# A 64-point transform centred on 31.5, so that the back-transform gives even and odd rows and one product gives a point and its mirror

## The chip, the cores and the metric

The kernel runs on one core of a Trainium2 chip. The metric is the device time of one execution in microseconds. Engines are named as in the profile: PE is the tensor engine's matmul, PEld its weight load, DVE the vector engine, ACT the scalar engine, POOL GpSimd, SP the engine whose queue issues most of the transfers.

## What is computed

```python
X = np.fft.rfft(x, axis=1)                       # x: 2 x 3008 x 256, float32
y = np.fft.irfft(X * (filt_r + 1j * filt_i)[None], n=3008, axis=1)
t = y.reshape(6016, 256)
g = t @ w_gate                                   # 256 x 1536
t = (g / (1 + np.exp(-g)) * (t @ w_val)) @ w_out # 1536 x 256
h = t @ w_in                                     # 256 x 2048
out = (h * np.clip(h + 3.0, 0.0, 6.0) / 6.0) @ w_out2
```

A long convolution along the sequence by way of the Fourier transform, and then two gated MLPs on the 6016 tokens that come out of it.

## The kernel before

**The transform.** 3008 is 47 x 64, and the two factors have no common divisor, so the transform splits into one of 47 points (N1) and one of 64 points (N2) without twiddle factors. Only 24 of the 47 frequencies of the first axis are kept (NK), since the input is real. The constants of all these transforms lie in one tile `mat` of 128 partitions, the same in both halves of 64 partitions.

The work runs in 16 steps (2 batches, 8 groups of 32 channels). A step `k` goes through four functions:

- `over_n1` (L414): the 47-point transform on PE, 32 products with 48 rows of contraction and 64 columns of weights; ACT copies the two result banks into `first` (L427, L428), with a negated copy of the real part.
- `over_n2` (L430): the 64-point transform on PE, eight products of 64 x 64 weights and 384 moving columns, four for the cosine and four for the sine, into two banks.
- `filter_product` (L440): DVE multiplies both banks with the real and the imaginary filter into `u` and `v` (L449, four operations of 384 elements); POOL then forms the complex product in place (four operations of 192 elements, through the helpers at L109 and L112).
- `back` (L455): the inverse 64-point transform on PE (L462). Its output rows are 64 real and 64 imaginary ones; each is the sum of a product with the cosine and one with the sine, so eight products of 64 x 64 weights and 384 moving columns. ACT copies the two banks into `turned` (L467).

The array is used as four parts of 64 x 64: a product with weights in rows 0 to 63 or 64 to 127 and results in partitions 0 to 63 or 64 to 127 takes one part, and up to four run beside each other.

The order is written out by hand. In iteration `k` PE's queue gets `over_n1(k)`, `back(k - 2)`, `over_n2(k)`, and in the last two iterations `form(k - 16)` in place of the transforms. The SP queue gets loads of x, filters and the first weights, then (L471) the stores of `turned` to DRAM (`d2`), then (L531) the loads of the first two blocks' data. DVE also decodes the first weights between the steps (`todo`).

**The last sum.** The tokens are worked on in blocks of 512 (the last of a batch 448): 12 blocks in all. For a block, `to_time` (L141) carries the 24 frequencies back to 47 points, on PE (L152). The data comes from DRAM with 48 rows (24 frequencies, real and imaginary) in partitions 0 to 47 for the first 32 values of n2 and the same in 64 to 111 for the other 32. The block's points fall into five to seven turns of at most 47 points. For each half of the channels (128 of 256) and each turn there are four products: two channel quarters of 64 columns, two halves of n2, each with 48 rows of contraction and up to 47 moving columns. They fill two PSUM banks, one for each half of n2. Two splits follow (`time_halves`, L157): ACT casts a bank to the high part of `xs`, DVE subtracts it to get the low part. One split reads both channel halves of its bank.

Blocks 0 and 1 get their last sum in `form` (L535), at the end of the transform stage; there the data of the two channel halves is loaded apart (`load_half`, L527). The other ten get theirs inside the first MLP's loop, at t = 2 * plain - 2 and then once in each block, between the block's `l1` products (L231) and the `l2` products (L243, or L253 in `l2_plain` for the first two blocks).

**The MLPs.** `l1` multiplies with the input weights (128 x 128 weights, 512 or 448 moving columns, in rounded float32 with the weights and the data as sums of two parts), `l2` with the output weights (a scheme of seven products for a 2 x 2 block, 256 or 224 moving columns; 21 products in a step). The order on PE is by hand here too.

Of the kernel before, what the change touches and what calls it, by code (L numbers as in the profile page):

```python
# [16 lines left out]
P = 128  # L17
B, S, D = 2, 3008, 256
N1, N2 = 47, 64
N1P = 48  # L20
NK = 24
# [4 lines left out]
BLOCKS = [(8 * j, min(8, N1 - 8 * j)) for j in range(6)]  # L26
# [20 lines left out]
def _token_times(time):  # L47

    order = []
    for j, n in BLOCKS:  # L50
        n = n * N2 // 2
        for r in range(2):
            q = 32 * j + np.arange(n)
            order.append(time[q % N1, 32 * r + q // N1])
    return np.concatenate(order)


M1, CO, SI, NS, FIN, NM = 0, 48, 112, 176, 240, 288


def _matrices():

    n1, k1, n2 = np.arange(N1), np.arange(NK), np.arange(N2)
    a = 2 * np.pi * (np.outer(n1, k1) % N1) / N1
    b = 2 * np.pi * (np.outer(n2, n2) % N2) / N2
    w = np.where(k1 == 0, 1.0, 2.0)[:, None] / S
    m = np.zeros((2, 64, NM))
    m[:, :N1, M1:M1 + NK] = np.cos(a)
    m[:, :N1, M1 + NK:M1 + 2 * NK] = -np.sin(a)
    m[:, :, CO:CO + N2] = np.cos(b)  # L70
    m[:, :, SI:SI + N2] = np.sin(b)
    m[:, :, NS:NS + N2] = -np.sin(b)
    m[:, 0:2 * NK:2, FIN:FIN + N1] = w * np.cos(a.T)
    m[:, 1:2 * NK:2, FIN:FIN + N1] = -w * np.sin(a.T)
    return np.ascontiguousarray(m.reshape(P, NM), np.float32)


@with_exitstack
def fft_conv_glu_mlp(ctx: ExitStack, tc: tile.TileContext, x, filt, mats, sgn, w1, w2, out):
    nc = tc.nc  # L80
# [9 lines left out]
    mat = keep.tile([P, NM], F32, name="mat")  # L90
# [14 lines left out]
    def bank(tag="gv"):  # L105
        return ps.tile([P, 512], F32, tag=tag, name=tag)

    def minus(out, a, b, engine=None):
        (engine or nc.vector).tensor_tensor(out=out, in0=a, in1=b, op=ALU.subtract)  # L109

    def plus(out, a, b, engine=None):
        (engine or nc.vector).tensor_tensor(out=out, in0=a, in1=b, op=ALU.add)  # L112
# [6 lines left out]
    def rows(i, n=64):  # L119

        return slice(i * 64, i * 64 + n)
# [8 lines left out]
    def load_g(b, j):  # L130
        t0, t1 = turns(*BLOCKS[j][:1], BLOCKS[j][1] * N2)
        g = new_g().rearrange("p (t c) -> p t c", c=D)
        for r in range(2):
            nc.sync.dma_start(out=g[rows(r, N1P), :t1 - t0],
                              in_=d2[b].rearrange("q (h n) c -> (q h) n c", h=2)[:, 32 * r + t0:32 * r + t1])
        return g[:, :, :P], g[:, :, P:]

# [3 lines left out]
    def to_time(g, j, tag="gv"):  # L141

        accs = [bank(tag), bank(tag)]
        first, n = BLOCKS[j][0], BLOCKS[j][1] * N2
        t0, t1 = turns(first, n)
        lo, hi = 32 * first, 32 * first + n // 2
        for a in range(2):
            for t in range(t0, t1):
                i0, i1 = max(lo, t * N1), min(hi, (t + 1) * N1)
                for o in range(0, P, 64):  # L150
                    for r in range(2):
                        nc.tensor.matmul(accs[r][o:o + 64, a * 256 + i0 - lo:a * 256 + i1 - lo],  # L152
                                         g[a][rows(r, N1P), t - t0, o:o + 64],
                                         mat[rows(r, N1P), FIN + i0 - t * N1:FIN + i1 - t * N1])
        return accs

    def time_halves(xs, accs, j, r):  # L157
        n = BLOCKS[j][1] * 32
        src = accs[r].rearrange("p (a n) -> p a n", a=2)[:, :, :n]
        return xs[:, 0, :, r * n:(r + 1) * n], xs[:, 1, :, r * n:(r + 1) * n], src  # L160

# [193 lines left out]
    with tc.manual_schedule():  # L357
# [10 lines left out]
        N = 16  # L368
        STEPS = [(b, 4 * a + i) for a in range(2) for b in range(B) for i in range(4)]
        xin, first, spec, acc2 = {}, {}, {}, {}  # L370
# [69 lines left out]
        def filter_product(k):  # L440

            us = mlp.tile([P, 8, 256], F32, tag="h", name="us").rearrange("p a b -> p (a b)")
            u = us[:, :4 * COLS].rearrange("p (o h n) -> p o h n", o=2, h=2)
            v = us[:, 4 * COLS:8 * COLS].rearrange("p (o h n) -> p o h n", o=2, h=2)
            f = fl[STEPS[k][1] // 4][:, k % 4].rearrange("p r (o n) -> p r o n", o=2)
            for o, acc in enumerate(acc2.pop(k)):
                xa = acc[:, :2 * COLS].rearrange("p (h n) -> p h n", h=2)
                for r, d in enumerate((u, v)):
                    nc.vector.tensor_tensor(out=d[:, o], in0=xa, op=ALU.mult,  # L449
                                            in1=f[:, r, o].unsqueeze(1).to_broadcast([P, 2, COLS]))  # L450
                minus(u[:, o, 0], u[:, o, 0], v[:, o, 1], nc.gpsimd)
                plus(u[:, o, 1], u[:, o, 1], v[:, o, 0], nc.gpsimd)
            spec[k] = u

        def back(k):  # L455

            accs, u = [bank(), bank()], spec.pop(k)
            for m in range(2):
                for h in range(2):
                    w, part = (CO, h) if m == 0 else ((NS, 1), (SI, 0))[h]  # L460
                    for r in range(2):
                        nc.tensor.matmul(accs[r][rows(h), :2 * COLS].rearrange("p (o n) -> p o n", o=2),  # L462
                                         mat[rows(r), w:w + N2], u[rows(r), :, part], start=m == 0, stop=m == 1)
            b, j = STEPS[k]
            to = turned.rearrange("p b q (j r o c) -> p b j r q o c", j=4, r=2, o=2)[:, b, j % 4]
            for r in range(2):
                nc.scalar.copy(out=to[:, r], in_=accs[r][:, :2 * COLS].rearrange("p (o c q) -> p q o c", o=2, q=NK))  # L467
# [59 lines left out]
        def load_half(j, a, g):  # L527
            t0, t1 = turns(*BLOCKS[j][:1], BLOCKS[j][1] * N2)
            g = g[:, :7 * P].rearrange("p (t c) -> p t c", c=P)
            for r in range(2):  # L530
                nc.sync.dma_start(out=g[rows(r, N1P), :t1 - t0],  # L531
                                  in_=d2[0].rearrange("q (h n) c -> (q h) n c", h=2)[:, 32 * r + t0:32 * r + t1, a * P:(a + 1) * P])
            return g

# [39 lines left out]
        hid, accs, late = {}, {}, {}  # L574
        base = 62

        for t in range(2 * n_pair):
            p, i = divmod(t, 2)
            k, g_ = steps[p]
            n, f = ntok(k), 2 * g_ + i  # L580
# [37 lines left out]
            h = hid[p].chunk(i)  # L618
            nc.scalar.activation(out=h, in_=hid[p].halves(gate), func=AF.Silu)  # L619

            lead, rest, part = ([f_ for f_ in range(2, F1) if t == 2 * f_ + d] for d in (-5, -4, -3))
# [23 lines left out]
            if i == 1 and (p == 0 or g_ == G1 - 1 and 0 < k < n_block - 2):  # L645
                j = 2 if p == 0 else k + 2
                gt[j] = load_g(*blocks[j])
            q, r = divmod(t - 2 * G1 - 8, 2)
# [12 lines left out]
            if t >= base:  # L661
                q, r = divmod(t - base, 4)
                if q < G2:
# [8 lines left out]
                    elif r == 3:  # L672
                        w = late[q].w.rearrange("p (s c) -> p s c", c=P)
# [29 lines left out]
            q = p - (n_pair - G1)  # L703
# [25 lines left out]
        for p in range(n_block * G2 + 2):  # L729
            k, g_ = divmod(p, G2)  # L730
            on = k < n_block

            if on:
                n = ntok(k)
# [19 lines left out]
            for i in range(2):  # L754
                if on:
                    h = hid["y", p].chunk(i)
# [72 lines left out]
```

## Time and profile before

| what | value |
|---|---|
| median of 3 runs | 1182.82 us (1180.63 to 1184.12) |
| the profiled execution's own time | 1181.04 us |
| its span, first to last instruction | 1179.2 us |
| mean granted clock of TensorE | 0.998 |
| PE busy | 1166.6 us, 99% |
| PEld busy | 1023.8 us, 87% |
| DVE busy | 1010.8 us, 86% |
| ACT busy | 611.9 us, 52% |
| POOL busy | 145.9 us, 12% |

A float32 product is two records of matmul and two of weight load. Busy time of PE counts pipelined matmuls whose ends are modelled, so the share alone does not say that PE is at its peak. The transform stage is roughly the first 75 us, the first MLP goes to about 636 us, the second from there to the end. In the chain, "issue" is time in which an engine waited for nothing that the profile shows. Mean durations of records include latency: records of several products overlap, so a rate is read from a group's time and its count.

### The profile page before, as it was taken

The numbers are of one execution on the slowest core, as the hardware profiler recorded it, in microseconds if no ns is written. First come the engines' busy times: TensorE is split into PE (matmuls) and PEld (weight loads), VectorE is DVE, ScalarE is ACT, GpSimd is POOL, SyncE is SP. The second block draws the span as 40 slices with busy tenths as digits, with TensorE's granted clock in tenths as the row PEclk, the third lists the DMA queues.
The fourth block names the chain that finished last, engine by engine and source line by source line (L and its number), as shares of the span: only waits on it lengthen the run. The fifth ranks groups of instructions, "written<-read, shape, count | busy, mean of one in ns | idle before, by whom it ended". The sixth has DMA issues, their size and how long they took to land.

```text
span 1179.2 us, 21833 instructions
## 1 busy us (share of the span) xinstructions
PE 1166.6 (99%) x9036; PEld 1023.8 (87%) x9036; DVE 1010.8 (86%) x1575; ACT 611.9 (52%) x928; POOL 145.9 (12%) x152
## 2 busy tenths in 40 slices
PE   9999999999999999999999999999999999999998
PEld 7778778888899888888889988899999999898997
DVE  5978877676678888778888899999999999999998
ACT  5553434343434444344445565656666566656654
POOL 4732310000002222012122300000000000000000
PEclk9999999999999999999999999999999999999999
DMA  9953500110113240312102211011001101100100
GB/s 305 300 155 96 148 21 36 24 36 19 21 59 83 83 109 24 96 47 71 43 12 99 63 35 36 1 37 36 23 13 37 34 1 36 37 15 23 34 18 17
DMA packets 43300, 70.32 MB, mean 60 GB/s; under 512 B 3712, under 2 KB 25088, under 8 KB 43200
## 3 DMA queue, kind: packets, MB, share of 16 engines
q1 hardware_dynamic: 42512, 68.17, 19.0%
q8 instruction: 71, 1.16, 0.4%
q10 hardware_dynamic: 688, 0.75, 0.2%
q14 instruction: 29, 0.24, 0.1%
HBM read 46.62 MB, written 22.28 MB: 58 GB/s over the span
## 4 chain that ended last, share of the span: by engine, by line
PE 91%; DVE 5%; DMA 1%; ACT 1%; issue 1%; POOL 1%; SPq 0%; ACTq 0%; DVEq 0%; POOLq 0%
PE gv L231 53%; PE a L243 31%; PE a L253 3%; DVE hs L109 2%; PE gv L152 1%; PE gv L462 1%; DVE h L759 1%; PE a L436 1%; PE gv L420 1%; DVE h L109 1%; ACT h L758 0%; DMA xin<-x_in 0%; POOL us L109 0%; DVE h L112 0%; DMA d<-turned 0%
## 5 line engine op out<-in xcount | busy, mean ns | idle before, releaser
L243 PEld LDWEIGHTS a<-hs,wall 128*128 128x128 f32 x3276 | 408.3, 189 | 13.6 <-issue 0.9
L243 PE MATMUL a<-hs,wall 128*128 128x256 f32 (+1 forms) x3276 | 414.4, 282 | 1.1 <-issue 0.5
L231 PE MATMUL gv<-xs,wall 128*128 128x512 f32 (+1 forms) x1728 | 407.5, 391 | 0.0
L231 PEld LDWEIGHTS gv<-xs,wall 128*128 128x128 f32 x1728 | 321.8, 189 | 64.9 <-ACT wall L491 0.3
L109 DVE TENSOR_TENSOR hs<-h,hs 128x768 fp32r<-128x768 f32 (+2 forms) x324 | 350.0, 1080 | 22.8 <-ACT hs L291 17.0
L231 PE MATMUL gv<-xs,wi 128*128 128x512 f32 (+1 forms) x1152 | 275.7, 388 | 0.0
L231 PEld LDWEIGHTS gv<-xs,wi 128*128 128x128 f32 x1152 | 210.1, 188 | 36.8
L302 ACT CAST hs<-h 128x1024 fp32r<-128x1024 f32 (+1 forms) x156 | 160.8, 1031 | 120.3 <-DVE h L109 120.1
L291 ACT CAST hs<-h 128x768 fp32r<-128x768 f32 (+1 forms) x156 | 128.1, 821 | 148.3 <-PE a L243 88.7
L109 DVE TENSOR_TENSOR h<-h 128x512 f32<-128x512 f32 (+3 forms) x312 | 184.5, 591 | 6.7
L628 DVE TENSOR_TENSOR h<-h,gv 128x512 f32<-128x512 f32 (+1 forms) x144 | 96.8, 672 | 54.9 <-PE gv L231 51.4
L759 DVE SCALAR_TENSOR_TENSOR h<-h,gv 128x512 f32<-128x512 f32 (+1 forms) x192 | 128.9, 672 | 16.0 <-ACT h L758 10.6
L758 ACT ACTIVATE h<-gv 128x512 f32<-128x512 f32 (+1 forms) x192 | 109.1, 589 | 62.9 <-PE gv L231 44.3
L619 ACT ACTIVATE h<-gv 128x512 f32<-128x512 f32 (+1 forms) x144 | 84.8, 589 | 88.4 <-PE gv L231 87.4
L112 DVE TENSOR_TENSOR h<-h 128x256 f32<-128x256 f32 (+1 forms) x156 | 65.8, 422 | 2.1
L112 POOL TENSOR_TENSOR ww<-ww,wa 128x512 f32<-128x512 f32 x16 | 20.7, 1297 | 368.3 <-issue 185.9
L253 PE MATMUL a<-hs,wall 128*128 128x512 f32 x144 | 36.7, 398 | 0.0
L253 PEld LDWEIGHTS a<-hs,wall 128*128 128x128 f32 x144 | 26.7, 188 | 8.1 <-DVE hs L109 2.2
L109 POOL TENSOR_TENSOR wall<-x,wall 128x512 fp32r<-128x512 f32 (+1 forms) x20 | 23.9, 1217 | 70.2 <-ACT wall L491 70.2
L462 PE MATMUL gv<-us,mat 64*64 64x384 f32 x256 | 28.9, 490 | 1.0 <-POOL us L109 0.4
L109 POOL TENSOR_TENSOR us<-us 128x192 f32<-128x192 f32 x32 | 26.0, 811 | 24.6 <-DVE us L449 23.3
L491 ACT CAST wall<-x 128x512 fp32r<-128x512 f32 x12 | 7.5, 623 | 40.0 <-DVE x L112 40.0
(79 smaller groups left out, 629.1 us busy)
## 6 DMA issues: line engine op xcount, KB each, us to landing
raw<-w_in SPq DMA_DIRECT2D x16, 512.0 KB, 4.4
xin<-x_in SPq DMA_DIRECT2D x30, 256.0 KB, 5.3
x<-w_in SPq DMA_DIRECT2D x9, 768.0 KB, 4.8
d<-turned SPq DMA_DIRECT2D x32, 192.0 KB, 4.9
yd<-y SPq DMA_DIRECT2D x10, 512.0 KB, 2.9
g<-yd SPq DMA_DIRECT2D x10, 512.0 KB, 3.8
y_out<-y SPq DMA_DIRECT2D x20, 256.0 KB, 2.3
wt<-wd SPq DMA_DIRECT2D x8, 448.0 KB, 3.4
```

Of the source, the lines that this page charges most:

```text
L109: (engine or nc.vector).tensor_tensor(out=out, in0=a, in1=b, op=ALU.subtract)
L112: (engine or nc.vector).tensor_tensor(out=out, in0=a, in1=b, op=ALU.add)
L231: nc.tensor.matmul(acc[:, :n], w[:, r, k * P:(k + 1) * P], xs[:, v, k, :n], start=(r, v, k) == (0, 0, 0), stop=(r, k) == (1, 1))
L243: nc.tensor.matmul(acc[b][:, 256 * h:256 * h + nt], w[:, r, iw], hs[:, v, ih, :nt], start=first and h == 0 and v == 0 and r == 1, stop=las ...
L253: nc.tensor.matmul(acc[j], w[:, r, ((0, 1), (3, 2))[j][i]], hs[:, v, 2 * i:2 * i + 2], start=first and (v, i, r) == (0, 0, 1), stop=last a ...
L291: nc.scalar.copy(out=self.parts(0, 0, 3), in_=v(1, 4))
L302: nc.scalar.copy(out=self.parts(0, 3, 7), in_=self.values(4, 8))
L462: nc.tensor.matmul(accs[r][rows(h), :2 * COLS].rearrange("p (o n) -> p o n", o=2), mat[rows(r), w:w + N2], u[rows(r), :, part], start=m == ...
L619: nc.scalar.activation(out=h, in_=hid[p].halves(gate), func=AF.Silu)
L628: nc.vector.tensor_tensor(out=h, in0=h, in1=hid[p].halves(val), op=ALU.mult)
L758: nc.scalar.activation(out=h, in_=pre, func=AF.Relu, bias=3.0)
L759: nc.vector.scalar_tensor_tensor(out=h, in0=h, scalar=6.0, in1=pre, op0=ALU.min, op1=ALU.mult)
```

## The change

The 64-point transform is taken about the middle of its points, 31.5: `n2 - 31.5` in place of `n2`. The cosine is then even and the sine odd under the mirror n2 -> 63 - n2. So the back-transform needs only 32 rows of the cosine and 32 of the sine: one product with 64 columns of weights (`EO`) gives the even sum of a part in 32 rows and the odd sum in 32. For each of real and imaginary part that is one product where there were two to be added, so four products a step in place of eight. Even and odd, real and imaginary are kept apart through DRAM, in as many bytes as before.

In the last sum the 96 rows (24 frequencies, real and imaginary, even and odd) are summed in one product, with 128 channels as the columns of weights. Its moving operand has the constants for the point and, with the sign of two terms turned, those for its mirror. So a turn and a channel half take one product with 96 rows, 128 columns of weights and up to 2 x 47 moving columns, in place of four. The second half of the points now comes in mirrored order (`_token_times`). The two banks now hold a channel half each, and so do the splits. The loaded rows lie in partitions 0 to 95.

In the last step (k = 15) POOL's four operations are left out, and `back` sums `u` and `v` itself in eight products, with a negated copy of the constants (`NE`). `mat` grows from 288 to 400 columns.

```diff
-            order.append(time[q % N1, 32 * r + q // N1])
+            order.append(time[q % N1, abs(63 * r - q // N1)])
...
-M1, CO, SI, NS, FIN, NM = 0, 48, 112, 176, 240, 288
+M1, CO, SI, EO, NE, FIN, NM = 0, 48, 112, 176, 240, 304, 400
...
-    b = 2 * np.pi * (np.outer(n2, n2) % N2) / N2
+    b = np.pi * (np.outer(2 * n2 - N2 + 1, n2) % (2 * N2)) / N2
...
-    m[:, :, NS:NS + N2] = -np.sin(b)
-    m[:, 0:2 * NK:2, FIN:FIN + N1] = w * np.cos(a.T)
-    m[:, 1:2 * NK:2, FIN:FIN + N1] = -w * np.sin(a.T)
-    return np.ascontiguousarray(m.reshape(P, NM), np.float32)
+    m[:, :, EO:EO + 32] = np.cos(b.T[:, :32])
+    m[:, :, EO + 32:EO + 64] = np.sin(b.T[:, :32])
+    m[:, :, NE:NE + 64] = -m[:, :, EO:EO + 64]
+    m = m.reshape(P, NM)
+    re, im = w * np.cos(a.T), -w * np.sin(a.T)
+    for r, sign in enumerate((1, -1)):
+        f = slice(FIN + r * N1, FIN + (r + 1) * N1)
+        m[0:2 * NK:2, f], m[1:2 * NK:2, f] = re, im
+        m[2 * NK:4 * NK:2, f], m[2 * NK + 1:4 * NK:2, f] = sign * im, -sign * re
+    return np.ascontiguousarray(m, np.float32)
...
-            nc.sync.dma_start(out=g[rows(r, N1P), :t1 - t0],
+            nc.sync.dma_start(out=g[r * N1P:(r + 1) * N1P, :t1 - t0],
...
+        final = mat[:2 * N1P, FIN:FIN + 2 * N1].rearrange("p (r n) -> p r n", r=2)
         for a in range(2):
+            to = accs[a][:, :n].rearrange("p (r n) -> p r n", r=2)
             for t in range(t0, t1):
                 i0, i1 = max(lo, t * N1), min(hi, (t + 1) * N1)
-                for o in range(0, P, 64):
-                    for r in range(2):
-                        nc.tensor.matmul(accs[r][o:o + 64, a * 256 + i0 - lo:a * 256 + i1 - lo],
-                                         g[a][rows(r, N1P), t - t0, o:o + 64],
-                                         mat[rows(r, N1P), FIN + i0 - t * N1:FIN + i1 - t * N1])
+                nc.tensor.matmul(to[:, :, i0 - lo:i1 - lo], g[a][:2 * N1P, t - t0, :],
+                                 final[:, :, i0 - t * N1:i1 - t * N1])
         return accs
 
-    def time_halves(xs, accs, j, r):
-        n = BLOCKS[j][1] * 32
-        src = accs[r].rearrange("p (a n) -> p a n", a=2)[:, :, :n]
-        return xs[:, 0, :, r * n:(r + 1) * n], xs[:, 1, :, r * n:(r + 1) * n], src
+    def time_halves(xs, accs, j, a):
+        n = BLOCKS[j][1] * N2
+        return xs[:, 0, a, :n], xs[:, 1, a, :n], accs[a][:, :n]
...
-                minus(u[:, o, 0], u[:, o, 0], v[:, o, 1], nc.gpsimd)
-                plus(u[:, o, 1], u[:, o, 1], v[:, o, 0], nc.gpsimd)
-            spec[k] = u
+                if k < N - 1:
+                    minus(u[:, o, 0], u[:, o, 0], v[:, o, 1], nc.gpsimd)
+                    plus(u[:, o, 1], u[:, o, 1], v[:, o, 0], nc.gpsimd)
+            spec[k] = u, v
...
-            accs, u = [bank(), bank()], spec.pop(k)
-            for m in range(2):
+            accs, (u, v) = [bank(), bank()], spec.pop(k)
+            sums = ((u, 0, EO), (u, 1, EO)), ((v, 1, NE), (v, 0, EO))
+            for m in range(1 if k < N - 1 else 2):
                 for h in range(2):
-                    w, part = (CO, h) if m == 0 else ((NS, 1), (SI, 0))[h]
+                    s, part, w = sums[m][h]
                     for r in range(2):
                         nc.tensor.matmul(accs[r][rows(h), :2 * COLS].rearrange("p (o n) -> p o n", o=2),
-                                         mat[rows(r), w:w + N2], u[rows(r), :, part], start=m == 0, stop=m == 1)
+                                         mat[rows(r), w:w + N2], s[rows(r), :, part],
+                                         start=m == 0, stop=m == 1 or k < N - 1)
```

## Rows read from the trace of the kernel before

**Rows 1.** The page: busy time, and the chain that ended last by engine.
```profile
PE 1166.6 (99%) x9036; PEld 1023.8 (87%) x9036; DVE 1010.8 (86%) x1575; ACT 611.9 (52%) x928; POOL 145.9 (12%) x152
...
PE 91%; DVE 5%; DMA 1%; ACT 1%; issue 1%; POOL 1%; SPq 0%; ACTq 0%; DVEq 0%; POOLq 0%
```
**Rows 2.** Windows by stage: busy us (count) of PE, PEld, DVE, ACT, POOL.
```profile
core 0: us, PE busy (x) PEld busy (x) DVE busy (x) ACT busy (x) POOL busy (x), PEclk, DMA share, GB/s
10.00:60.00 50.00, 47.89 (x1229) 35.94 (x1225) 42.79 (x73) 27.94 (x76) 36.74 (x53) 1.00 0.98 308
...
75.00:600.00 525.00, 524.86 (x3621) 449.77 (x3621) 413.31 (x627) 224.33 (x333) 77.99 (x73) 1.00 0.21 60
636.00:1160.00 524.00, 523.00 (x3299) 476.89 (x3298) 501.78 (x790) 321.29 (x450) 13.87 (x6) 1.00 0.10 32
```
**Rows 3.** Chain in order of time, transform stage: start us, us, what.
```profile
16.87 1.30 PE gv L462 x14
18.17 1.17 PE a L436 x15
19.34 1.05 PE gv L420 x56
...
24.54 0.60 POOL us L109
...
34.58 1.28 POOL us L112
```
**Rows 4.** Timeline of one step: start us, us, engine, line, operation.
```profile
17.55 0.48 ACT L427 COPY first<-gv 128x384 f32<-128x384 f32 x1
...
17.85 1.75 PE L436 MATMUL a<-first,mat 64*64 64x384 f32 x16
```
**Rows 5.** Chain in order of time, end of the transform stage.
```profile
56.88 0.80 ACT turned L467 x2
...
61.94 4.13 DMA d<-turned
...
69.87 0.83 PE a L152 x37
...
72.09 1.65 PE a L152 x85
73.74 1.36 issue
...
75.35 4.76 PE gv L231 x13
```
**Rows 6.** Windows, behind the last sum of block 1; 0.55 is PEclk.
```profile
75.40:79.20 3.80, 3.80 (x10) 3.02 (x11) 2.50 (x4) 0.57 (x1) 0.00 (x0) 0.55 0.02 4
```
**Rows 7.** Chain in order of time, inside the two MLPs.
```profile
446.39 2.49 PE a L243 x21
448.88 5.61 PE gv L231 x24
454.49 1.75 PE gv L152 x112
456.24 2.69 PE a L243 x21
...
605.60 1.31 PE gv L152 x80
...
1127.53 2.53 PE a L243 x21
...
1142.46 2.34 PE a L243 x21
```
**Rows 8.** Groups by form: busy us, mean ns of one | idle before.
```profile
L243 PEld LDWEIGHTS a<-hs,wall 128*128 128x128 f32 x3276 | 408.3, 189 | 13.6 <-issue 0.9 <-ACT hs L302 0.7 <-DVE y L325 0.5
...
L152 PEld LDWEIGHTS gv<-mat,g 48*64 48x64 f32 x992 | 15.4, 135 | 3.6 <-issue 3.6
...
L405 PE MATMUL gv<-turned 128*128 128x128 f32 x16 | 3.4, 402 | 1.1 <-DVE turned L399 1.1
```
**Rows 9.** Line 405 (idle products at the start): duration ns min/median/max.
```profile
L405 PEld LDWEIGHTS gv<-turned x16: 192/333/338, 1.1 to 4.1; 128*128 128x128 f32 x16
```

More of the change, by code (lines that the diff above doesn't have):

```diff
@@ L530, in load_half @@
             for r in range(2):
-                nc.sync.dma_start(out=g[rows(r, N1P), :t1 - t0],
+                nc.sync.dma_start(out=g[r * N1P:(r + 1) * N1P, :t1 - t0],
                                   in_=d2[0].rearrange("q (h n) c -> (q h) n c", h=2)[:, 32 * r + t0:32 * r + t1, a * P:(a + 1) * P])
```

## The prediction

> **What bounds the kernel now.** I read the page first. The tensor engine's matmuls are busy for 99% of the span, and the chain of work that ended last is 91% PE [rows 1]. So a change in PE's work should move the end, but only where PE itself is what the stage waits for. The windows by stage say where that is [rows 2]. From 75 to 600 us PE is busy 524.86 of 525 us, and DVE 413; from 636 to 1160 us PE 523.0 of 524. There each added or saved microsecond of PE is one of the end. From 10 to 60 us, in the transforms, PE has 47.9 of 50, but DVE has 42.8, POOL 36.7, and the DMA engines stand at 0.98. That stage has four near-bounds, and its own chain has to be read.
>
> The chain in order of time shows that stage's loop: back-transform 1.30 us, second transform 1.17, first transform 1.05, again and again [rows 3]. Between 24.5 and 35.9 us the same chain runs through POOL and DVE instead. One step's timeline shows a second path beside PE [rows 4]: ScalarE copies the second result bank of the first transform from 17.55 us on, and the second transform starts at 17.85. The 1.30 us of the back-transform, which runs meanwhile, is the cover of these copies.
>
> The end of the stage is a chain of its own [rows 5]: ScalarE copies, the store's transfer of 4.13 us, the load's, then the last sums of two blocks with a back-transform between them, then 1.36 us "issue", in which PE waited for nothing that is shown. After it the clock is 0.55 of full speed for 3.8 us, which is the 1.2 GHz level for nearly all of it [rows 6].
>
> The other ten last sums stand inside the MLP, in PE's order, at 1.31 us for 80 records to 1.75 us for 112; the group behind one takes 2.69 us, and others of the same 21 records 2.49 [rows 7].
>
> **The change part by part.** The sum is made on the profiled execution, 1181.04 us (span 1179.2 and 1.8 around it). The median of the runs shown is 1.8 us above it, and I add that at the end.
>
> *Last sum, inside the MLP.* Before, a turn (up to 47 points) and channel half takes four 64-column products, each two records of weights and two of matmul. The view by form counts 992 records in the MLP [rows 8], so 124 such groups. The rows 1.31 and 1.75 give 13.75 ns for each further record and 0.21 fixed, so blocks of 96 records take 1.53; four of 1.75, four of 1.53 and two of 1.31 are 15.7 us. With 0.20 behind each (2.69 − 2.49) the ten cost 17.7 us. Blocks of 6 and of 7 turns have the same 256 points in a half, and still differ by 0.22 us: the price goes by products, not by points.
>
> After, a group is one product with 128 columns of weights and 2 × 47 moving columns, so 124 products and 248 records. No row has this shape, so it gets two bounds. Below: the moving columns alone. The back-transform streams 384 columns twice in 1.30 us [rows 3], 1.69 ns a column; the ten blocks have 4992 columns in each half, so 2 × 4992 × 1.69 ns = 16.9 us, 68 ns a record. Above: the records of L243, which also have 128 × 128 weights, come every 2.53/21 = 120 ns with 256 moving columns, 29.9 us in all. The row nearest is L243 with 224 moving columns: 2.34/21 = 111 ns [rows 7]. I take it, though 94 columns stream in less, because of the weights: a load of 64 columns is on record for 135 ns, one of 128 for 189, or 192 in L405's smallest [rows 8, 9], so 64 more columns add about 55 ns and 128 occupy about 110 ns, whatever streams. In the old form the four array parts load side by side. So 248 × 111 ns = 27.6 us against 17.7: **+9.9**, between −0.8 and +12.2. Here a wide product is dearer than four narrow ones beside each other.
>
> The Trainium skill has a rule that speaks against the change in the same way: "TensorE: Matmul & The Clock Gate", section "LDWEIGHTS (loading the stationary operand)", counts only columns, P/1.2 ns, 107 ns for 128 by its figure. By it the ten blocks would take an estimated 26.5 us, and the term would be +8.8; the 55 ns between the rows of 64 and 128 columns agree.
>
> The 0.20 behind each block I count as gone, since full-width products then stand beside full-width products. If it stays, it is 2.0 us more. The Trainium skill, "TensorEngine Tiling (Array Packing)", "Key Properties", says that changing the tiling drains the engine; the 2.69 against 2.49 agrees with that, and no row shows whether 96 rows count as a change.
>
> *Last sum of blocks 0 and 1.* One half of block 0 is done while the load is awaited. On the chain are 6 + 12 groups, 0.83 + 1.65 us [rows 5]. After: 36 records at 111 ns are 4.0 us, **+1.5** (+0.1 at the stream, +1.9 at 120 ns), and I add **0.2** for the change of shape to the back-transform between.
>
> *The stall and the low clock.* The 1.36 us "issue" lies within the last sum of block 1, where 16 instructions pass in about 125 ns. With a quarter of them I expect the instruction supply to keep up: **−1.4**, ends 0 and −1.4. The low clock followed an idle PE. It costs 4.76 us for 13 records [rows 5]; at 5.61/24 each [rows 7] they take 3.04, so 1.7. It may come again, for the wait for the load stays; I take half, **−0.9**, ends 0 and −1.7.
>
> *Back-transform.* For 15 of 16 steps four products instead of eight: 1.30 becomes 0.65. Eleven lie ahead of the point, near 55 us, where the chain leaves PE, so at most 11 × 0.65 = 7.2 us. But the cover of ScalarE's copies goes with it. The second transform's second bank is ready at about 18.03 (17.55 + 0.48), and two rounds of 0.64 us behind that end near 19.3; before, it ended at 19.34 [rows 3, 4]. So a step of this kind gains 0.1, and the steps bound by POOL and DVE nothing: **−1.1**, ends 0 and −7.2. The step ahead of the stores is already ScalarE's [rows 5].
>
> *At nothing.* The last step leaves out POOL's four operations and sums in PE instead: it runs behind block 0's sum, with its eight products as before. The splits of a block read a whole bank of one channel half, the same 512 elements; they may start earlier, and PE waits for none of them. The constants grow by 57 KB, which at 308 GB/s is **+0.2** ahead of the first product; no queue is moved.
>
> Sum: 9.9 + 1.7 − 2.3 − 1.1 + 0.2 = +8.4; 1189.4 on the profiled scale, 1191.2 on that of the median.
>
> **The rivals.**
> - *A, the load hides.* One mechanism, the other sign: weights of 128 columns load within the 68 ns in which the mean record streams. Then the last sums are −0.8 and +0.1, and the sum is −0.8 + 0.3 − 2.3 − 1.1 + 0.2 = −3.7: 1179.1. For it: PE would have fewer, fuller products, and nothing records a 128-column load without a long stream over it. Against it: the 55 ns, and L243, whose records fall only to 111 ns at 224 columns. It decides below about 75 ns a record ((17.7 + 2.5 + 1)/284).
> - *B, the transforms are PE's after all.* The whole 7.2 us comes back, because copies and POOL move up too. Sum 8.4 − 6.1 = +2.3: 1185.1. For it: most of the loop's chain reads PE. Against it: the copies at 17.55, DVE's 42.8 of 50, DMA at 0.98.
> - *C, load and stream add up.* L405 has 128-column f32 weights and 128 moving columns, and its 16 records take 3.4 us, 215 ns each [rows 8]. At that price the ten blocks cost 53.3 us and the first two 7.7: +35.6 and +5.5, about 1219. Against it: its loads are 333 ns at the median and 192 at the least [rows 9], so most of it was at a lower clock than the rows around it tell.
>
> **How the numbers follow.** The likeliest, with weights at 107 to 120 ns, gets 0.68, and its own range is 1186 to 1197 (+2.0 for the drain, +2.3 if stall and clock come back; −1.1 at 107 ns, some of B). A gets 0.13, B 0.10, C 0.04, A with B (about 1173) 0.03; 0.02 is left for others. The range 1182 to 1198 takes the likeliest and B, and leaves out A and C. Within 0.3% (3.5 us: about what a measurement of this kernel can tell from no change) is 1179.3 to 1186.4: most of B, half of A, a little of the likeliest, 0.17. Slower: most of the likeliest, C and some of B, 0.72. Faster: half of A, A with B and the rest, 0.11.
>
> **What would show it.** In the chain, a last sum inside the MLP: 12 products and 24 records in about 2.7 us (A: 1.7; C: 5.2), and the group of 21 records behind it at 2.49. L462 falls from 256 records to 136. The first product of the MLP starts near 74 us against 75.35 before, with ScalarE's copies on the chain of the transforms (B: near 68). No 1.36 us "issue" ahead of it. I am wrong if the record of a last sum is under 75 ns, or if the transforms shorten by more than 3 us.

## The result, and the profile after

The changed kernel takes 1195.01 us in the median of 5 runs (1192.72 to 1196.55), the kernel before 1183.4 (1180.63 to 1185.89) beside it. The ratio is 1.0094, 95% interval 1.0076 to 1.0112: slower by 0.9%, forecast +0.7% (1191.2, range 1182 to 1198). The profiled execution is the slowest of the five, 1196.55 us, with a span of 1194.8 against 1179.2.

The page of the changed kernel, answering to [rows 1]: PE stays at 99% of a longer span, with 1008 fewer records of matmul.

```profile
PE 1181.1 (99%) x8028; PEld 1032.4 (86%) x8028; DVE 1010.6 (85%) x1575; ACT 612.8 (51%) x928; POOL 142.7 (12%) x148
...
PE 90%; DVE 4%; DMA 3%; ACT 1%; issue 1%; SPq 1%; ACTq 0%; DVEq 0%
```

Its chain in order of time inside the MLP, answering to [rows 7] (L158 is the last sum, L235 `l1`, L247 `l2`):

```profile
457.93 2.50 PE a L247 x21
460.42 5.58 PE gv L235 x24
466.00 3.05 PE gv L158 x28
469.05 2.58 PE a L247 x21
...
620.40 2.21 PE gv L158 x20
```

A last sum of seven turns has 28 records for 112 and takes 3.05 us for 1.75; one of five turns 2.21 for 1.31. Per record that is 109 and 110 ns, and again the price goes by products: 28, 24 (2.61 to 2.64 us) and 20 records lie near one line, although blocks of 28 and of 24 records move the same 512 columns in each channel half. The ten together are 27.1 us for 15.7. The group behind takes 0.04 to 0.09 more than its like, where it took 0.20 more.

The groups by form of the changed kernel, answering to [rows 8], show the load of 96 rows and 128 columns at 192 ns. A record of matmul with 10 moving columns lasts 237 ns and one with 94 lasts 279; these durations include latency, and records overlap:

```profile
L158 PEld LDWEIGHTS gv<-mat,g 96*128 96x128 f32 x248 | 29.3, 192 | 0.8
...
L158 PE MATMUL gv<-mat,g 96*128 96x94 f32 x180 | 24.0, 279 | 0.0
...
L158 PE MATMUL gv<-mat,g 96*128 96x10 f32 x8 | 1.3, 237 | 0.0
```

The chain at the end of the transform stage, answering to [rows 5] (L468 is `back`, L478 the stores, L538 the loads), and two windows, answering to [rows 6] (busy us and count of PE, PEld, DVE, ACT, POOL, then the granted clock):

```profile
62.62 4.30 DMA d<-turned
...
67.44 2.96 DMA g<-d
70.40 0.09 issue
70.49 2.48 PE a L158 x12
72.98 2.77 PE gv L468 x16
...
75.74 5.34 PE a L158 x24
```
```profile
66.00:70.40 4.40, 1.37 (x12) 1.25 (x12) 2.79 (x6) 1.49 (x4) 0.00 (x0) 1.00 0.50 119
70.80:84.40 13.60, 13.60 (x61) 10.77 (x60) 3.87 (x6) 2.62 (x5) 0.00 (x0) 0.50 0.17 57
```

The load lands at 70.4 us, 0.6 later than before. The 1.36 us "issue" is gone. But PE was busy for only 1.37 of the 4.40 us ahead of 70.40 (its wait for the load is 3.1 us, where it was 0.6), and from 70.8 to 84.4 us its clock is at 0.50, the 1.2 GHz level, though it is busy all that time. The three pieces on PE last twice as long as at the 2.4 GHz level (a run below shows them there), and the MLP's first product starts at 81.1 us, against 75.35. From there to the end the changed kernel takes 1194.8 − 81.1 = 1113.7 us, the kernel before 1179.2 − 75.35 = 1103.9: the MLP costs 9.9 more, and the rest of this execution's 15.6, that is 5.7, is the end of the transforms. The medians are only 11.6 apart: the profiled execution of the changed kernel is 1.5 above its median, and that of the kernel before 2.4 below. The mean clock is 0.994 in this execution, 0.995 in one of the others and 0.996 in three.

### The profile page after: what moved, and what is told of

Read it like the earlier page. It is cut to its first block, busy times and chain, and to the rows that moved or that the text cites. A ratio compares the mean times of both kernels' runs of the same rounds, so it can differ in the third digit from the quotient of the medians.

```text
span 1194.8 us, 19803 instructions
## 1 busy us (share of the span) xinstructions
PE 1181.1 (99%) x8028; PEld 1032.4 (86%) x8028; DVE 1010.6 (85%) x1575; ACT 612.8 (51%) x928; POOL 142.7 (12%) x148
## 4 chain that ended last, share of the span: by engine, by line
PE 90%; DVE 4%; DMA 3%; ACT 1%; issue 1%; SPq 1%; ACTq 0%; DVEq 0%
PE gv L235 52%; PE a L247 30%; PE a L257 3%; PE gv L158 2%; DVE hs L115 2%; DMA d<-turned 1%; DVE h L766 1%; DMA x<-w_in 1%; DMA xin<-x_in 1%; PE a L440 1%; PE a L158 1%; PE gv L468 1%; DVE h L115 1%; PE gv L424 1%; ACT h L765 0%
## 5 line engine op out<-in xcount | busy, mean ns | idle before, releaser
L247 PEld LDWEIGHTS a<-hs,wall 128*128 128x128 f32 x3276 | 408.4, 189 | 13.1 <-issue 0.9
L247 PE MATMUL a<-hs,wall 128*128 128x256 f32 (+1 forms) x3276 | 414.2, 282 | 1.0 <-issue 0.5
L235 PE MATMUL gv<-xs,wall 128*128 128x512 f32 (+1 forms) x1728 | 407.6, 391 | 0.0
L235 PEld LDWEIGHTS gv<-xs,wall 128*128 128x128 f32 x1728 | 321.9, 189 | 65.0 <-ACT wall L498 0.5
L235 PE MATMUL gv<-xs,wi 128*128 128x512 f32 (+1 forms) x1152 | 275.7, 388 | 0.0
L235 PEld LDWEIGHTS gv<-xs,wi 128*128 128x128 f32 x1152 | 210.1, 188 | 36.8
L440 PE MATMUL a<-first,mat 64*64 64x384 f32 x240 | 30.9, 493 | 0.2 <-ACT first L431 0.2
L158 PEld LDWEIGHTS gv<-mat,g 96*128 96x128 f32 x248 | 29.3, 192 | 0.8
L158 PE MATMUL gv<-mat,g 96*128 96x94 f32 (+7 forms) x248 | 28.7, 271 | 0.0
```

The source lines that it names most:

```text
L158: nc.tensor.matmul(to[:, :, i0 - lo:i1 - lo], g[a][:2 * N1P, t - t0, :], final[:, :, i0 - t * N1:i1 - t * N1])
L235: nc.tensor.matmul(acc[:, :n], w[:, r, k * P:(k + 1) * P], xs[:, v, k, :n], start=(r, v, k) == (0, 0, 0), stop=(r, k) == (1, 1))
L247: nc.tensor.matmul(acc[b][:, 256 * h:256 * h + nt], w[:, r, iw], hs[:, v, ih, :nt], start=first and h == 0 and v == 0 and r == 1, stop=las ...
```

## The experiments

Theory: a record of the last sum takes the time of its load of 128 columns; the halved back-transform brings the end nothing, since ScalarE's copies, the transfers and then a longer wait take it back; that wait brings the low clock. The rivals: A (moving columns set the record), B (the transforms did gain), and the clock falling because of the wide products. Ratios are to the kernel before on the same chip.

**The two halves of the change apart.** First the new `back` with the old last sum:

```diff
-                nc.tensor.matmul(to[:, :, i0 - lo:i1 - lo], g[a][:2 * N1P, t - t0, :],
-                                 final[:, :, i0 - t * N1:i1 - t * N1])
+                for o in range(0, P, 64):
+                    for r in range(2):
+                        nc.tensor.matmul(accs[r][o:o + 64, a * 256 + i0 - lo:a * 256 + i1 - lo],
+                                         g[a][rows(r, N1P), t - t0, o:o + 64], mat[rows(r, N1P), ...])
```

> The changed kernel's back-transform (four products a step) with the old last sums (four products of 64 columns for each turn and channel half, two splits over both banks). The even and odd sums are then not brought together into points, so the numbers that leave it are not the convolution's; all counts and sizes are those of the two kernels. Theory (the copies by ScalarE set the loop's pace, so the halved back-transform brings nothing to the transforms; the wide products cost): the ten sums in the MLP are back at 1.3 to 1.75 us, the loop's step stays at 3.65 us, the MLP's first product starts between 74 and 78 us, total 1181 to 1186. Rival (the halved back-transform does shorten the transforms, and the changed kernel lost that at the end of the stage): first product near 70 us, total near 1177.

Measured: 1181.4 us, ratio 0.9995 (0.9982 to 1.0007). The last sums in the MLP are those of before to the hundredth (1.75, 1.53, 1.31). In the early steps `back` starts at 17.61 and 21.25 us, 3.64 apart: half of its products are gone, and the loop is no faster. PE waits 3.3 us for the load of block 0, and a low clock of 0.72 on average over 66 to 84 us follows; the MLP's first product starts at 78.3. B falls: the steps are as long as before, and the load lands no earlier (71.6 us). A gain could hide behind the low clock in this profile, but it is that of the slowest of ten executions, with a mean clock of 0.995; the others have 0.997 or 0.998, near the 0.998 to 1.000 of the kernel before, and took 1179.6 to 1183.6 us, not 1177.

Then the old `back`, with POOL in all steps, and the new last sum:

```diff
-            for m in range(1 if k < N - 1 else 2):
+            for m in range(2):
```

> The changed kernel's last sums with the old back-transform (eight products a step, POOL's operations in all 16). Full sums are then taken for even and odd ones, so the result is not the convolution's; counts and sizes are unchanged. Theory: it is as slow as the changed kernel, 1192 to 1196, with 3.04 us for each last sum of 28 records, since all of the loss is in the last sums and the clock at the end of the transforms. Rival (the halved back-transform brought a gain that hides a larger loss): 1198 or more. Other rival (the back-transform's change caused the long wait and so the low clock): 1189 to 1191, with the low clock no longer than 3.4 us.

Measured: 1192.6 us, ratio 1.0098 (1.0077 to 1.0119). The end of the stage in this run (chain in order of time, and a window):

```profile
68.87 2.06 PE gv L466 x16
70.92 2.80 PE a L158 x24
73.73 1.45 PE gv L466 x16
75.18 2.84 PE a L158 x24
```
```profile
66.00:84.00 18.00, 17.91 (x141) 12.86 (x139) 13.27 (x21) 9.19 (x19) 5.83 (x8) 1.00 0.32 93
```

PE has no wait for the load, the clock stays at 1.00, and a last sum of 24 records takes 2.80 us. The time is the theory's; the low clock is gone in this profile as the other rival had it, though its total of 1189 to 1191 was missed. So within the intervals the whole cost sits in the last sum. The long low clock comes with both halves together: the five executions of the changed kernel have mean clocks of 0.994 to 0.996, while nine of ten with the halved `back` alone have 0.997 or more, and three of four with the wide products alone 0.999 or more (the fourth has 0.995, at 1196.2 us).

**What a record of the last sum waits for.** Half of the moving columns:

```diff
-                nc.tensor.matmul(to[:, :, i0 - lo:i1 - lo], g[a][:2 * N1P, t - t0, :],
-                                 final[:, :, i0 - t * N1:i1 - t * N1])
+                nc.tensor.matmul(to[:, 0, i0 - lo:i1 - lo], g[a][:2 * N1P, t - t0, :],
+                                 final[:, 0, i0 - t * N1:i1 - t * N1])
```

> The changed kernel, but each product of the last sum moves only the up to 47 columns of the points, not of their mirrors; the splits read the same columns twice. The mirrored points are left out. Weights and the number of products stay. Theory (a record is as long as its load of 128 columns of weights): a last sum of 28 records stays at 2.9 to 3.05 us, total within 2 us of the changed kernel. Rival (a record is set by its moving columns, with a fixed part): with half the columns 28 records take about 2 us and the total falls by 8 to 10 us.

Measured: 1197.4 us, ratio 1.0131 (1.0116 to 1.0146). The chain shows the same last sums with 47 moving columns as with 94:

```profile
263.86 3.03 PE gv L158 x28
...
621.18 2.17 PE gv L158 x20
```

A falls: the moving columns do not set the record. The total is 2.4 us above the changed kernel (4.4 by the ratios) and not within 2, because something else came. Behind three of the last sums the clock went to the lower level, as this window behind the first one shows (0.51 is the granted clock). The groups behind these three took 4.5 us more than in the changed kernel (4.33, 4.10 and 4.11 us for 2.88, 2.58 and 2.58):

```profile
169.00:175.10 6.10, 6.10 (x42) 5.47 (x41) 3.25 (x4) 2.26 (x4) 0.00 (x0) 1.00 0.00 0
175.10:178.60 3.50, 3.50 (x11) 2.82 (x11) 2.33 (x7) 0.58 (x1) 0.00 (x0) 0.51 0.65 142
```

Then each product as two of 64 columns, beside each other in the two column halves of the array:

```diff
-                nc.tensor.matmul(to[:, :, i0 - lo:i1 - lo], g[a][:2 * N1P, t - t0, :],
-                                 final[:, :, i0 - t * N1:i1 - t * N1])
+                for o in range(0, P, 64):
+                    nc.tensor.matmul(to[o:o + 64, :, i0 - lo:i1 - lo], g[a][:2 * N1P, t - t0, o:o + 64],
+                                     final[:, :, i0 - t * N1:i1 - t * N1])
```

> The changed kernel with each product of the last sum taken as two of 64 columns of weights, beside each other in the two column halves of the array, all else as it is; the result is the same convolution. Theory (a record of the last sum is as long as its load, the load goes by its columns, and loads into different parts of the array run beside each other, as in the kernel before): a group then takes the 2 x 78 ns of its moving columns in place of 2 x 111, a last sum of 28 records' worth falls from 3.04 to about 2.2 us, the ten from 26.9 to about 19 us, total 6 to 9 us less, 1186 to 1189. Rival (one load at a time, whatever part it goes to): the sum of the columns is the same, 3.0 us stay, total as the changed kernel.

Measured: 1185.2 us, ratio 1.0020 (1.0008 to 1.0033). Its chain, and its loads by form:

```profile
447.24 2.49 PE a L248 x21
449.73 5.58 PE gv L236 x24
455.31 2.20 PE gv L159 x56
457.51 2.69 PE a L248 x21
```
```profile
L159 PEld LDWEIGHTS gv<-mat,g 96*64 96x64 f32 x496 | 19.3, 137 | 3.6 <-issue 3.3 <-ACT h L627 0.3
```

Twice the records with the same columns of weights in all, in 2.20 us for 3.05. The loads are 55 ns shorter (137 for 192), and 56 of them one behind the other at half of 109 ns would take 3.05 us, so the loads of the two halves run beside each other. This settles the term. A product of the changed kernel, now a pair, falls from 218 ns to 157 in the mean. The expectation explained that by the 94 moving columns, but the mean does not: blocks of seven turns take 2.20 us and blocks of six 1.94 to 1.98, though both move 512 columns in each channel half. An estimate from rows fits all ten blocks within 0.03 us: 0.2 us fixed, and for each pair 1.69 ns a moving column (the back-transform's rate) but at least 109 ns, twice half a record of the changed kernel. By it a full turn of 94 columns is set by its moving columns and a short one still by its load. The group behind takes 2.69 again, 0.20 more than its like.

**The low clock.** Idle products in the wait for the load:

```diff
+            if a == 1 and fill:
+                fill()
...
-            acc = to_time(gt[j], j, "a")
+            acc = to_time(gt[j], j, "a", (lambda: keep_busy(13)) if j == 0 else None)
+        def keep_busy(n):
+            acc = bank()
+            for _ in range(n):
+                nc.tensor.matmul(acc[:, :P], mat[:, :P], mat[:, :P])
```

> The changed kernel with 13 idle products of 128 x 128 on the constants in PE's queue between the two channel halves of block 0's last sum, where PE waited 3.12 us for a load. Theory (the 3.12 us of idle PE led to the low clock, which lasted 13.65 us over the last sums of blocks 0 and 1 and cost about 6.8): the clock stays at 2.4 GHz, the chain's pieces 2.48, 2.77 and 5.34 us become about 1.3, 1.3 and 2.7, total 5 to 7 us less than the changed kernel, 1188 to 1190. Rival (the clock falls because the wide products themselves keep the array too little busy): the clock falls a little later all the same, total within 2 us of the changed kernel.

Measured: 1192.35 us, ratio 1.0084 (1.0069 to 1.0099). That is 2.7 us below the changed kernel's median, less than the 5 to 7 expected of a run as slow as the profiled one, and by the ratios 1.2 us, which the intervals do not tell from nothing. The chain:

```profile
68.24 1.46 PE a L160 x12
69.70 2.98 PE gv L547 x26
72.68 1.27 PE a L160 x12
73.94 1.45 PE gv L470 x16
75.39 2.84 PE a L160 x24
78.23 11.19 PE gv L237 x48
```

The 2.48, 2.77 and 5.34 us are 1.27, 1.45 and 2.84, and the granted clock is 1.00 from 66 to 84 us. With the wide products kept and only the wait filled, the clock stays. So here the wide products alone do not bring the low clock; it follows the idle wait. Why it then lasts so long is open: the halved `back` with the old sums had a wait of 3.3 us, and in most of its executions no long low clock. The idle products have a price of their own: they end at 72.68 us, and the load, issued near 68.6 and 2.9 us on its way, lands near 71.5 (an estimate).

Both remedies together:

> Both the two 64-column products and the 13 idle products. Theory: the two gains lie in different places and add, 1183 to 1187. Rival (the idle products gain nothing once the last sums are short, as the end of the stage is then set by the load alone): as the two halves alone.

Measured: 1184.15 us, ratio 1.0010 (1.0000 to 1.0021). The gain over the two halves alone is within the intervals. In the profile of those, PE waits 2.5 us and the clock stays at 1.00 from 66 to 84 us without idle products. So in that execution there was no low clock to remove; the mean clock of the ten is 0.996 to 0.999, against 0.998 to 1.000 here. That the load sets the end was not tested apart.

**What took back the halved back-transform.** The 47-point transform one step ahead, to cover ScalarE's copies:

```diff
-            if 1 < k < N:
-                over_n1(k)
+            if 0 < k < N - 1:
+                over_n1(k + 1)
```

> The changed kernel with the 13 idle products that keep the clock up, and with the 47-point transform one step ahead in PE's queue, so that a whole step lies between it and the 64-point transform and ScalarE's copies are covered (the odd steps' copies lie in a buffer that is free until step 12). Theory (the cover of ScalarE's copies is what took back the halved back-transform): the loop's step falls from 3.65 us to 3.2 to 3.4 in the early steps, and the MLP's first product starts 1 to 4 us earlier than in the run with idle products alone, total 1188 to 1191. Rival (DVE, POOL and the transfers hold the pace at the same level): the step stays at 3.6 us, total as with the idle products alone, 1192.

Measured: 1198.78 us, ratio 1.0139 (1.0117 to 1.0160), slower than either theory. The chain, and what PE waited for between 8 and 60 us (us in total, times, the longest):

```profile
32.39 0.66 PE gv L470 x7
33.05 1.26 PE a L442 x15
34.32 0.89 PE gv L426 x60
...
35.26 0.66 PE gv L470 x7
35.92 1.26 PE a L442 x15
37.19 0.89 PE gv L426 x60
...
38.82 6.90 DMA xin<-x_in
```
```profile
PE gv L426 <- issue: 8.2, 4, 4.0
PE gv L426 <- DMA xin<-x_in: 2.0, 5, 0.8
```

Where its data is there, a step takes 35.26 − 32.39 = 2.87 us. The copies were the limit of the single step, as the prediction had it. The 6.90 us are the way of one load of x from issue to landing; PE was busy for 5.81 of them, and it never waited more than 0.8 us for x, 2.0 in all. What PE lost is 8.2 us of "issue", in four pieces of up to 4.0, where the run with idle products alone has 1.4; the mean clock from 10 to 60 us is 0.90. So the next expectation starts from a wait for x that was not there.

With the two halves of the last sum as well, 

> The two 64-column products, the idle products and the 47-point transform one step ahead together. Theory: 1180 to 1185, at or just below the kernel before (1182.7). Rival (transfers hold the stage's pace): as without the step ahead, 1183 to 1187.

Measured: 1190.99 us, ratio 1.0068 (1.0049 to 1.0087): again some 7 us slower than without the step ahead. The next three issue the loads of x a step earlier too:

```diff
-            send(k, load_x, k + 3)
+            send(k - 1, load_x, k + 3)
```

> The run with the 47-point transform one step ahead was 6 us slower than with the idle products alone, although its step fell from 3.65 to 2.87 us wherever its data was there: it waited for loads of x of 6 to 7 us, since each load was issued as late as before and used a step earlier. Here each load of x is issued a step earlier too. Theory (the wait came from the later issue, and the copies' cover is what the loop lacks): the waits of several us for x go, the loop's step is 2.9 to 3.4 us, total 1187 to 1191. Rival (the transfers are at their limit, so that any faster loop waits for them): the waits stay or move to the filters, total 1192 or more, as with the idle products alone (1192.4) or slower.

> The changed kernel with two 64-column products in place of one in the last sum, the 47-point transform one step ahead and the loads of x a step earlier, without idle products. Theory: the two halves alone came to 1185.2; 1 to 5 us less, 1180 to 1184. Rival (transfers at their limit): 1185 or more.

> The kernel before, with the 47-point transform one step ahead and the loads of x a step earlier, its back-transform and last sums as they were. Theory (with eight products of the back-transform PE is busy 3.5 us a step, so the cover is already paid): the step stays at 3.5 to 3.65 us, total within 2 us of the kernel before. Rival (transfers at their limit, or a wait for the earlier loads): slower by 2 us or more.

Measured: 1196.97 us, ratio 1.0123 (1.0104 to 1.0142); 1193.3, ratio 1.0090 (1.0071 to 1.0110); 1191.62, ratio 1.0079 (1.0062 to 1.0096). All three are slower than their like without the step ahead, even the kernel before with its eight products. The DMA share from 10 to 60 us is 0.92, 0.92 and 0.91, below the 0.98 of [rows 2], so these runs do not show a stage at the transfers' limit. They show "issue" pieces of 0.2 to 2.1 us inside the 47-point transform (5.5 to 7.0 us in all), and in the last four steps ScalarE's copies in the open (only one buffer was left there, since the other holds a block's data by then). The second of them, without idle products, has a low clock as well: 0.53 from 60 to 66 us, 0.78 from 66 to 84. As a remedy the step ahead failed for reasons of its own, and as a test of the stage's limit it is inconclusive.

The last one leaves PE's order and the loads alone, and has ScalarE copy both banks ahead of the negated copies (with the two 64-column products):

```diff
-            for r in range(2):
-                acc = accs[r][:, :2 * COLS].rearrange("p (c h q) -> p c h q", h=2, q=NK)
-                nc.scalar.copy(out=first[k][:, r, :, 0:2], in_=acc)
-                nc.scalar.mul(out=first[k][:, r, :, 2], in_=acc[:, :, 0], mul=-1.0)
+            for r in range(2):
+                nc.scalar.copy(out=first[k][:, r, :, 0:2], in_=acc[r])
+            for r in range(2):
+                nc.scalar.mul(out=first[k][:, r, :, 2], in_=acc[r][:, :, 0], mul=-1.0)
```

> The changed kernel with two 64-column products in place of one in the last sum, and with ScalarE's four copies of a step in another order: both banks of the first transform first, then both negated copies, so that the second bank is ready about 0.35 us earlier (the loads and PE's order are as they were). Theory (what the halved back-transform left uncovered is the wait for the second bank's copy): the loop's step falls from 3.65 us in the early steps by 0.2 to 0.35 us, and the stage ends up to 3 us earlier unless the loads and stores at its end hold it; total 1182 to 1185.5, against 1185.2 with the two halves alone. Rival (the step is held by something else, DVE, POOL or the transfers): the step stays at 3.65 us.

Measured: 1184.53 us, ratio 1.0005 (0.9992 to 1.0018); the two halves alone had 1.0020 (1.0008 to 1.0033). ScalarE's copies into `turned`, one pair a step, where the loop is steady, first of this run, then of the changed kernel (timeline):

```profile
26.17 0.89 ACT L476 COPY turned<-gv 128x384 f32<-128x384 f32 x2
29.60 0.89 ACT L476 COPY turned<-gv 128x384 f32<-128x384 f32 x2
33.02 0.90 ACT L476 COPY turned<-gv 128x384 f32<-128x384 f32 x2
```
```profile
25.55 0.89 ACT L474 COPY turned<-gv 128x384 f32<-128x384 f32 x2
29.20 0.89 ACT L474 COPY turned<-gv 128x384 f32<-128x384 f32 x2
32.84 0.89 ACT L474 COPY turned<-gv 128x384 f32<-128x384 f32 x2
```

The step is 3.42 to 3.43 us, against 3.64 to 3.65 (with the two halves alone 3.65 to 3.66). So the theory holds: in a steady step the wait for the second bank's copy is the limit, and the order of the copies is worth 0.2 us. In the profile it reaches nothing at the end: PE waits 3.3 us for block 0's load, which lands near 70.2 us as before. The total is not told apart from that of the two halves alone.

## Why the prediction was right, and where a term was not

**The last sum in the MLP: right in mechanism and size.** Forecast +9.9 from 111 ns a record, measured +9.9 over the whole MLP, from 109 to 110 ns. The half of the moving columns and the two halves of the weights show that the load sets it. The rule of the Trainium skill, "TensorE: Matmul & The Clock Gate", section "LDWEIGHTS (loading the stationary operand)", 107 ns for 128 columns by its figure, is near the measured 109 to 110 as well. The extra time behind a last sum was counted as gone: 0.04 to 0.09 of 0.20 us stays. In the run with 64-column products it is 0.20, so it goes with the partition into columns; that it is a drain was not shown. For blocks 0 and 1 the forecast was +1.5; with the clock kept they take 1.27 + 2.84 us for 0.83 + 1.65, +1.6.

**The stall at the end of the transforms: gone, as forecast.** The 1.36 us does not appear ahead of the MLP in the changed kernel, nor in the run with the old `back` and the new last sum. That it was the instruction supply was only argued, but the traces speak for it. Counted from the start, the PE and PEld records ahead of the "issue" pieces of 0.2 us or more in front of PE are 445, 1965, 2218, 2725 and, at the 1.36 us, 3485 in the kernel before; 1205, 1965, 2218 and 2725 with the old `back` and the new last sum; 951, 1711 and 2723 in the changed kernel. Neighbours lie some 253 records apart or a multiple of it, whatever line PE is in. So these pieces stand at places in the order of instructions, not at a kind of work. At many such places none is seen, and no run was made to test the reason.

**The low clock: the term that failed.** The step gave it −0.9, between 0 and −1.7: it could only stay or go. It grew from 3.4 us (0.55 over 3.8 us, [rows 6]) to 13.6 in the profiled execution. The work in that stretch is dear at the lower level: last sums and a back-transform that take 10.6 us there take 5.6 with the clock kept. The step named the wait for the load as a reason for the low clock to come again, but took the wait as it stood. It did not ask what happens to the wait itself when PE arrives earlier and the load does not: PE stood ready 1.9 us earlier (67.4 us for 69.3), the load landed 0.6 later, and the wait went from 0.6 us to 3.1. The MLP's first product, forecast near 74 us, starts at 81.1.

**The back-transform: −1.1 forecast, not borne out; the reason, the copies, was right.** The steps keep 3.65 us (16.50, 20.15), as the copies' cover said; the 0.1 a step that the forecast left is not there either. The batch's last copy ahead of the stores ends at 56.39 us where it ended at 57.68, which looks like the −1.1, but that is chance: the same transforms end that copy at 57.4 us with the old last sums and at 57.8 with the two halves, and 1.1 of the 1.3 us arise in two steps from 41 to 49 us, where the kernel before took 4.13 and 4.28 us and this one 3.69 and 3.66. The 1.3 us were lost again in the SP queue. It was busy with loads until 57.7 and issued the first of the eight stores at 58.01 (57.70 before), and the chain shows one of the eight held, for 0.2 us, until 59.79 by an earlier store's landing:

```profile
53.55 6.24 DMA d<-turned
59.79 0.02 issue
59.80 1.09 SPq L478
```

So the term ended at nothing, its upper bound. The prediction said of the added constants that no queue is moved; for the back-transform it did not ask what the queue does when the data is ready sooner.

The sum for the end of the transforms was −1.5 and the profiled execution has +5.7. The medians give about +1.7 (11.6 − 9.9). With the clock kept the median is +9.7; in that profile the MLP's first product starts at 78.23 us, 2.9 later than before, and from there to the end it takes 8.2 us more, not 9.9, because the 1.7 us of low clock at the MLP's start are gone too. So that +9.7 comes near the MLP's +9.9 because other terms cancel. The forecast of the difference came out 3.2 us low (+8.4 for +11.6): the clock went the other way, and the −1.1 of the back-transform is not there. It came out inside its range because the large term was right.

**Rivals.** A is refuted by the half of the moving columns, C by 110 ns a record against its 215. B is refuted by the steps of the new `back` with the old last sums, which stay 3.64 us apart, and by its 1181.4 us, where the expectation put B near 1177. (The 1219 for C stands on the scale of the profiled execution, the totals of A and B on that of the median; C is 1220.7 there.)

## What to carry to other kernels

Count what a small product loads as well as what it moves. Here a product with 128 columns of weights took about 218 ns with up to 94 moving columns and with half of them, and at 1.69 ns a column it would take 129 moving columns to fill that time (an estimate); below that, in float32, one wide product can be dearer than narrow ones beside each other in parts of the array, since the parts load at the same time. When an engine is made faster ahead of a wait for a transfer, price the longer wait: here PE came earlier, the load did not, and a low clock followed that cost some 5 us in the profiled execution. Before crediting a shorter product, look at what ran in its shadow: here the copies that it covered kept the step at 3.65 us. And read a long transfer in a chain as the transfer's own time; how long an engine stood still for it is in the waits.

## What the runs showed of the hardware that was not expected

- PE at the lower clock does not have to be idle: from 70.8 to 84.4 us it was busy 13.60 of 13.60 us at 0.50, in last sums, a back-transform and the first products of the MLP.
- With 47 moving columns behind loads of 128, the clock fell behind three of the ten last sums, though nothing waited (0.51 from 175.1 to 178.6 us); with 94 columns it fell behind none.
- After waits of much the same length the clock fell in some runs (2.4 us with half the moving columns, 3.1, 3.3) and not in another (2.5 us with the two 64-column products).
- The "issue" pieces in front of PE in the transforms stand at counts of PE and PEld records that are 250 to 254 or a multiple of it apart, in ten profiles and in whatever line, with 0.2 to 4.0 us each. One of 0.95 us at the last step's back-transform, in four runs with the 47-point transform ahead, does not fit.
